# A planned three-stage kernel: where the copies of gate's and val's blocks run, when down 2's first job is made, and how the planner books its transfers

## Chip, core and metric

The kernel runs on one core of one Trainium2 chip. The metric is the device time of one execution in microseconds, given as the median of several runs.

## The reference, cut to what matters

```
x   = attention(q, k, v, omega)            # 2304 tokens x 512, kernelized attention, 4 x 8 heads
h   = x @ w_in                             # 512 -> 2048              "up 1"
x   = (h * sigmoid(h)) @ w_out             # 2048 -> 512              "down 1"
g   = x @ w_gate ; v = x @ w_val           # 512 -> 1536, twice       "up 2"
out = (g * sigmoid(g) * v) @ w_out2        # 1536 -> 512              "down 2"
```

All of it is in float32, so a matrix product is made from three products of rounded float32 (fp32r) parts: a value is split into a high part (a copy that rounds) and a low part (the value less its high part).

## The kernel before

After attention, the four large products run one after the other on TensorE: up 1, down 1, up 2, down 2. Each is a 2 x 2 block product with seven products in place of eight (`PROD`, `ORDER`), so each operand is needed as seven blocks, four of them or fewer straight from memory and the others sums of these.

**Tiles.** Up 2 walks 36 tiles n in the order of `up_order`: for each pair i of weights (gate i and val i, i = 0 to 5) and each of three column ranges s, gate's tile and then val's. One tile is seven products of six matmuls (128 x 128 by 384 columns). Products of neighbouring tiles are interleaved: product 1 of tile n+1 runs between product 7 and product 3 of tile n. Between products, `copy` (line 1123) moves a bank of PSUM to another on ScalarE, and a later product starts on that bank; `add` (line 1180), `post` (lines 1147 and 1164) and `put` (line 1132) finish a block and store it to `g_d`. Each result sits in one of ten slots (`f_s`) from its ScalarE copy until its store has landed.

**Weights.** They come as 64-bit words, and `conv_job` turns one block of weights into operands. A job has two loads (line 330), then for each half a step on ScalarE (`first`, line 352) and two on VectorE (`shift`, line 359, and `low`, line 366), then four sums on GpSimd (line 385). A job of in, gate or val goes on to four copies `hi` and four subtractions `lo` (line 432): the copies of parts 1 and 2 (512 columns each) run on VectorE (line 417), those of part 0 (256 columns) and part 3 (512 columns) on ScalarE (line 419). A job of out or out2 (`down_job`) instead stores its seven blocks to memory in three stores (line 449), and the down product loads them later (line 1285). `weave` interleaves the tail of one job with the head of the next. In up 2 the jobs stand in the order down 0, gate 1, val 1, down 1, gate 2, val 2, down 2, and so on to gate 5, val 5, down 5; gate 0 and val 0 were made in up 1 and are loaded from memory.

**Buffers.** A job takes two raw buffers (`f_raw`), two `f_c`, one `f_sum` and, for gate or val, two of six weight slots (`f_w`). Gate 0 and val 0 hold four of the weight slots when up 2 begins. The other two lie where the raw columns of the last range of x are (`T_AT`) and come free when `x_prep(1, 2)` has been emitted (`close_z`, called from `hook2`); gate 0's two come free after tile 4. The raw, `f_c` and `f_sum` buffers lie in `fa`, where down 1's operands lie before (`ZP`).

**The order of the work** is written by a planner when the kernel is built. `clk` holds an expected time for each engine, `T` one for each result. Between two products `flush` emits what it believes ready: results' work first, then the streams z, split, wd, x and conv, each no further ahead than its `ahead`. Each engine then runs its own instructions strictly in the order in which they were emitted, SyncE (all transfers) too, and waits in front of the first one that isn't ready. So the books decide the order, and real waits decide the time. A transfer is booked by `dma_cost` as bytes / 350e3 us, one after the other, plus 3.0 us.

Of the kernel before, what the change touches and what calls it, by code (L numbers as in the profile page):

```python
# [42 lines left out]
def kernel(  # L43
# [15 lines left out]
    P = 128  # L59
# [18 lines left out]
    N = 384  # L78
    NSB = NT // (2 * N)
    FP = (w_in.shape[0], w_gate.shape[0])  # L80
# [20 lines left out]
    def cut(t, o, n):  # L101
        return t[:, o : o + n]
# [36 lines left out]
                return  # L139
            self.q.append((x, clk["PE"] if t is None else t))  # L140

    clk = {e: 0.0 for e in ("PE", "ACT", "DVE", "POOL", "SP", "dma", "slot")}
    T = {}
    fixed = {"ACT": (0.21, 0.00081), "DVE": (0.15, 0.00106), "POOL": (0.25, 0.0021), "COPY": (0.1, 0.0006)}

    def cost(kind, n):
        a, b = fixed[kind]
        return a + b * n

    class Op:  # L150
# [22 lines left out]
        def emit(self):  # L173
            t = max(clk[self.eng], self.ready())
            clk["slot"] = 0.0
            clk["end"] = t + self.cost
            self.fn()
            if self.eng == "SP":
                clk["SP"] = t + 0.3
                clk["dma"] = max(t, clk["dma"]) + self.cost  # L180
                end = clk["dma"] + 3.0
            else:
                clk[self.eng] = end = t + self.cost
            for k in self.outs:
                T[k] = end
            if self.then is not None:
                self.then(end)

    def dma_cost(nbytes):
        return nbytes / 350e3  # L190

    urgent = []
    maker = {}
# [123 lines left out]
    f_s = Free("s", s_slots)  # L317
# [5 lines left out]
    def conv_job(kind, i, dram=None, side=False):  # L323
        b = {}
        key = lambda *k: (kind, i, *k)

        def load(h):
            def go():
                b["r", h] = r = f_raw.take()
                nc.sync.dma_start(out=r.bitcast(U32), in_=wsrc[kind][i, h])  # L330

            def then(end):

                if kind == "out2":
                    T[key("r", h)] = end + 6.0

            return Op("SP", dma_cost(P * 4096), go, outs=[key("r", h)], slots=(f_raw, 1), then=then)

        def word(h, w):
            return b["r", h].bitcast(U32).rearrange("p (c w) -> p c w", w=2)[:, :, w]  # L340
# [60 lines left out]
        def done(t):  # L401
            f_c.give(b["c", 0], t)
            f_c.give(b["c", 1], t)
            f_sum.give(b["S"], t)
# [5 lines left out]
        def hi(k):  # L410
            def go():
                if ("w", 0) not in b:
                    b["w", 0], b["w", 1] = f_w.take(), f_w.take()
                if side:
                    nc.gpsimd.tensor_scalar(dst(0, k), src(k), 1.0, 1.0, op0=ALU.mult, op1=ALU.mult)
                elif k in (1, 2):
                    nc.vector.tensor_copy(dst(0, k), src(k))
                else:
                    nc.scalar.activation(dst(0, k), src(k), AF.Copy)

            n = 256 * (parts[k][1] - parts[k][0])
            eng, c = ("DVE", cost("COPY", n)) if k in (1, 2) else ("ACT", cost("ACT", n))
            if side:
                eng, c = "POOL", cost("POOL", n)
            return Op(
                eng, c, go, ins=[key(*x) for x in after[k]], outs=[key("hi", k)],
                slots=lambda: None if ("w", 0) in b else (f_w, 2),
            )
# [13 lines left out]
        def store(a, z, src, ins):  # L442

            b["stores"] = 3

            def go():
                o = dram(a, z)
                t = src()
                nc.sync.dma_start(out=o, in_=t.rearrange("p (o c) -> p o c", c=256) if len(o.shape) == 3 else t)
                b["stores"] -= 1  # L450
                if not b["stores"]:
                    done(clk["end"] + 2.0)

            return Op("SP", dma_cost(P * (z - a) * 1024), go, ins=[key(*x) for x in ins], outs=[key("d", a)])

        half = [load(0), load(1), first(0), first(1), shift(0), low(0), shift(1), low(1)]
        if dram is not None:
# [51 lines left out]
    def down_job(m, i):  # L509
        k = DNK[m]  # L510
        return conv_job(
            k, i, dram=lambda a, z: wd_d[k][a:z, :, i * 256 : (i + 1) * 256].rearrange("o p c -> p o c")
        )
# [34 lines left out]
    def x_prep(m, s, raws, temps, eng, early=False, before=None, after=(), then=None):  # L548
# [9 lines left out]
        def load(j, n):  # L558
            k, h = n

            def go():
                r[n, j] = t = raws(j, 2 * k + h)
                if m == 0:
                    t0 = (2 * s + h) * N
                    for c, a, z, _, _ in runs(t0, t0 + N):
                        o = t0 + a - c * S
                        nc.sync.dma_start(out=t[:, a:z].bitcast(F32), in_=x_d[c][2 * k + j][:, o : o + z - a])
                else:
                    nc.sync.dma_start(out=t.bitcast(F32), in_=x2_d[s, 2 * k + h, j])

            if m:
                ins = [("x2", s, 2 * k + h, j), *after]
            else:
                t0 = (2 * s + h) * N
                ins = [("xd", c, 2 * k + j) for c, *_ in runs(t0, t0 + N)]
            if before is not None:
                ins = ins + [("x", m, before, "lo", n, j) for n in ("B11", "T1", "T2", "B21", "B22", "T3", "T4")]
            return Op("SP", dma_cost(P * N * 4), go, ins=ins, outs=[key(n, j)])

        def hi(name, of, j, after):  # L580
            def go():
# [494 lines left out]
    def up_phase(m, seq, hook):  # L1076
# [50 lines left out]
        def put(n, c, t, key):  # L1127
            i, kind, s = seq[n]
            f = i + (FP[m] if c & 2 else 0)

            def go():
                nc.sync.dma_start(out=g_d[m][s, c & 1, f], in_=t)
                f_s.give(t, clk["end"] + 2.0)

            soon("SP", dma_cost(P * N * 4), go, ins=[key], outs=[("g", m, s, c & 1, f)])

# [144 lines left out]
    def split_load(take, n, src, key, slots, ins=(), parts=1):  # L1281


        def load():
            nc.sync.dma_start(out=cut(take()[1], 0, n).bitcast(F32), in_=src)

        def hi(o, w):
            h, l = (cut(t, o, w) for t in take())
            nc.scalar.activation(h, l.bitcast(F32), AF.Copy)

        def lo(o, w):
            h, l = (cut(t, o, w) for t in take())
            nc.vector.tensor_sub(l, l.bitcast(F32), h.bitcast(F32))  # L1293

        def then(end):
            T[key("r")] = end + 2.0

        ops = [Op("SP", dma_cost(P * n * 4), load, ins=ins, outs=[key("r")], slots=slots, then=then)]
        w = n // parts
        for o in range(0, n, w):  # L1300
            end = [key()] if o + w == n else []
            ops += [
                Op("ACT", cost("ACT", w), lambda o=o: hi(o, w), ins=[key("r")], outs=[key("hi", o)]),
                Op("DVE", cost("DVE", w), lambda o=o: lo(o, w), ins=[key("hi", o)], outs=[key("lo", o), *end]),
            ]
        return ops

    def zload(m, s, n, k, after=()):
        fp = FP[m]
        a, h = HB[n]  # L1310
        f = a * fp + 2 * k

        def go():
            nc.sync.dma_start(
                out=ZP[n](768 * k, 768).rearrange("p (f n) -> p f n", f=2).bitcast(F32),
                in_=g_d[m][s, h, f : f + 2].rearrange("f p n -> p f n"),
            )

        return Op(
            "SP", dma_cost(2 * P * N * 4), go, ins=[("g", m, s, h, f), ("g", m, s, h, f + 1), *after], outs=[("z", m, s, n, k)],  # L1320
            guard=lambda: not len(streams["conv"]),
        )

    def down_phase(m, Wd, hook, until=None):
# [67 lines left out]
        def out_(s, c, e, t, key):  # L1392

            k, h = divmod(c, 2)

            def go():
                if m == 0:
                    nc.sync.dma_start(out=x2_d[s, c, e], in_=t)
                else:
                    t0 = (2 * s + h) * N  # L1400
                    nc.sync.dma_start(out=outT[(2 * k + e) * P : (2 * k + e + 1) * P, t0 : t0 + N], in_=t)
                f_s.give(t, clk["end"] + 2.0)

            soon("SP", dma_cost(P * N * 4), go, ins=[key], outs=[("x2", s, c, e)])

# [133 lines left out]
    def more():  # L1539

        f_c.give(extra_c)
        f_raw.give(extra_raw)
# [82 lines left out]
    for _ in d1:  # L1625
        pass
    f_w.q = deque(sorted(f_w.q, key=lambda x: x[1]))
    streams["x"].extend(x_prep(1, 2, lambda j, c: cut(ra, T_AT + (4 * j + c) * N, N), True, "DVE"))
    jobs = [down_job(1, 0)]
    for i in range(1, FP[1]):  # L1630
        jobs += [conv_job("gate", i), conv_job("val", i), down_job(1, i)]

    conv2 = weave(*jobs)
    seq2 = up_order(("gate", "val"), FP[1], False, False)
# [2 lines left out]

    def hook2(n, p):
        if n == 0 and p == 1:
            more()  # L1640
            streams["conv"].ahead = 0.8
            streams["conv"].extend(conv2)
        if not len(streams["x"]):
            close_z()
        if n == len(seq2) - 5 and p == 1:
            streams["wd"].extend(wd_ops2)
            streams["z"].extend(z_first(1, "B11", "B12"))
            streams["split"].extend(next(d2))
# [56 lines left out]
```

## Time and profile before

| | us |
|---|---|
| median of 3 runs | 840.74 (839.5 to 844.63) |
| the profiled execution, its own time | 842.8 |
| its span, first to last instruction | 841.0 |
| TensorE matmul busy | 819.3 |
| VectorE busy | 623.3 |
| ScalarE busy | 549.0 |
| GpSimd busy | 167.3 |

A span is one execution on the hardware profiler's clock; the time around it (1.8 us here) is start and end. Stages by the order of lines in the trace: attention to 118 us, up 1 to 294 us, down 1 to 459.5 us, up 2 to 714 us, then down 2.

### The profile page before, as it was taken

The numbers are of one execution on the slowest core, as the hardware profiler recorded it, in microseconds if no ns is written. First come the engines' busy times: TensorE is split into PE (matmuls) and PEld (weight loads), VectorE is DVE, ScalarE is ACT, GpSimd is POOL, SyncE is SP. The second block draws the span as 40 slices with busy tenths as digits, with TensorE's granted clock in tenths as the row PEclk, the third lists the DMA queues.
The fourth block names the chain that finished last, engine by engine and source line by source line (L and its number), as shares of the span: only waits on it lengthen the run. The fifth ranks groups of instructions, "written<-read, shape, count | busy, mean of one in ns | idle before, by whom it ended". The sixth has DMA issues, their size and how long they took to land.

```text
span 841.0 us, 18097 instructions
## 1 busy us (share of the span) xinstructions
PE 819.3 (97%) x6889; PEld 795.4 (95%) x6889; DVE 623.3 (74%) x1016; ACT 549.0 (65%) x1166; POOL 167.3 (20%) x204
## 2 busy tenths in 40 slices
PE   8999899999999999999999998999999999999998
PEld 7888789999899999999998997999999999999998
DVE  4888777667663699895999988574757548997772
ACT  6999878866677866454567865555556547755552
POOL 0477741035441000000000035121314010000000
PEclk9999999999999999999999999999999999999999
DMA  8688956669899977528415657362627168764502
GB/s 282 190 272 279 280 192 229 202 199 323 287 335 337 354 273 215 161 64 240 148 63 188 206 157 232 120 212 97 227 87 236 55 208 281 253 207 130 175 15 76
DMA packets 110119, 170.08 MB, mean 202 GB/s; under 512 B 9424, under 2 KB 94032, under 8 KB 110032
## 3 DMA queue, kind: packets, MB, share of 16 engines
q1 hardware_dynamic: 109808, 168.69, 61.2%
q8 instruction: 54, 0.88, 0.4%
q14 instruction: 33, 0.27, 0.1%
q10 hardware_dynamic: 224, 0.23, 0.1%
HBM read 107.02 MB, written 61.87 MB: 201 GB/s over the span
## 4 chain that ended last, share of the span: by engine, by line
PE 77%; DMA 7%; DVE 5%; ACT 5%; issue 3%; POOL 2%; SPq 0%; ACTq 0%; DVEq 0%; POOLq 0%
PE ps L1106 35%; PE ps L1485 32%; PE ps L760 4%; PE ps L804 2%; DMA fa<-in_moe_w_out 2%; PE ps L820 2%; PE ps L851 2%; POOL fa L385 2%; DMA wd_out<-fa 2%; ACT kq L776 2%; DMA g_d<-fa 1%; DVE fa L366 1%; ACT ps L1123 1%; ACT fa L1147 1%; DVE ra L432 1%
## 5 line engine op out<-in xcount | busy, mean ns | idle before, releaser
L385 POOL TENSOR_TENSOR fa<-fa 128x256 f32<-128x256 f32 x124 | 107.8, 884 | 494.0 <-DVE fa L366 283.3
L1106 PE MATMUL ps<-ra 128*128 128x384 f32 x840 | 148.3, 328 | 7.0 <-ACT ps L1123 6.4
L1106 PE MATMUL ps<-rb,ra 128*128 128x384 f32 x840 | 146.2, 327 | 2.9 <-ACT ps L1123 2.9
L1106 PEld LDWEIGHTS ps<-ra 128*128 128x128 f32 x840 | 137.6, 189 | 9.9 <-ACT ps L1123 8.9
L1106 PE MATMUL ps<-rc,ra 128*128 128x384 f32 x840 | 145.7, 326 | 1.1 <-ACT ps L1123 1.0
L1106 PEld LDWEIGHTS ps<-rb,ra 128*128 128x128 f32 x840 | 137.7, 189 | 4.3 <-ACT ps L1123 4.1
L1106 PEld LDWEIGHTS ps<-rc,ra 128*128 128x128 f32 x840 | 137.7, 189 | 2.1 <-ACT ps L1123 2.0
L1123 ACT ACTIVATE ps<-ps 128x384 f32<-128x384 f32 x180 | 85.1, 476 | 66.7 <-PE ps L1106 62.9
L1180 DVE TENSOR_TENSOR fa<-fa,ps 128x384 f32<-128x384 f32 x120 | 66.3, 552 | 81.6 <-ACT ps L1123 58.6
L1340 ACT ACTIVATE ra<-fa 128x768 fp32r<-128x768 f32 x87 | 73.1, 843 | 63.4 <-PE ps L1485 57.3
L1344 DVE TENSOR_TENSOR ra<-fa,ra 128x768 fp32r<-128x768 f32 x87 | 83.1, 957 | 20.2 <-ACT ra L1340 18.1
L1485 PE MATMUL ps<-ra,rb 128*128 128x384 f32 x528 | 87.5, 326 | 0.5 <-DVE rb L1293 0.5
L1485 PEld LDWEIGHTS ps<-ra,rb 128*128 128x128 f32 x528 | 86.0, 189 | 0.8 <-DVE rb L1293 0.8
L776 ACT ACTIVATE kq<-ps,nb 128x128 f32<-128x128 f32 x288 | 79.4, 405 | 7.9 <-DVE nb L774 7.6
L1485 PE MATMUL ps<-ra,rc 128*128 128x384 f32 x486 | 80.9, 327 | 1.4 <-DVE ra L1344 1.4
L1485 PEld LDWEIGHTS ps<-ra,rc 128*128 128x128 f32 x486 | 79.0, 189 | 2.3 <-DVE ra L1344 2.1
L1485 PE MATMUL ps<-ra 128*128 128x384 f32 x486 | 80.3, 326 | 0.0
L1485 PEld LDWEIGHTS ps<-ra 128*128 128x128 f32 x486 | 79.2, 189 | 0.0
L352 ACT ACTIVATE fa<-fa 128x512 f32<-128x512 f32 x65 | 53.8, 828 | 22.5 <-DMA fa<-in_moe_w_gate 5.7
L1364 DVE TENSOR_TENSOR fa<-ra,fa 128x768 f32<-128x768 f32 x63 | 60.1, 954 | 0.7
L1147 ACT ACTIVATE fa<-fa 128x384 f32<-128x384 f32 x84 | 43.6, 519 | 24.8 <-DVE fa L1180 24.7
L366 DVE SCALAR_TENSOR_TENSOR fa<-fa 128x512 uint32<-128x512 uint32 x65 | 55.0, 846 | 0.7
(108 smaller groups left out, 1086.0 us busy)
## 6 DMA issues: line engine op xcount, KB each, us to landing
g_d<-fa SPq DMA_DIRECT2D x168, 192.0 KB, 4.1
fa<-g_d SPq DMA_DIRECT2D x42, 384.0 KB, 4.5
ra<-g_d SPq DMA_DIRECT2D x42, 384.0 KB, 3.9
fa<-in_moe_w_out SPq DMA_DIRECT2D x28, 512.0 KB, 5.2
fa<-in_moe_w_in SPq DMA_DIRECT2D x16, 512.0 KB, 5.3
wd_out<-fa SPq DMA_DIRECT2D x12, 512.0 KB, 3.2
fa<-in_moe_w_gate SPq DMA_DIRECT2D x12, 512.0 KB, 4.0
fa<-in_moe_w_val SPq DMA_DIRECT2D x12, 512.0 KB, 5.1
```

The costliest lines, as they stand in the source:

```text
L352: nc.scalar.activation(c, word(h, 1).bitcast(F32), AF.Prelu, scale=2.0**-112, alpha=-(2.0**32))
L366: nc.vector.scalar_tensor_tensor(c, word(h, 0), 29, c, op0=ALU.logical_shift_right, op1=ALU.bitwise_or)
L385: f(blk(f"S{n}"), blk(l), blk(r))
L776: nc.scalar.activation(e[:, g // 2, g % 2, h * M : (h + 1) * M], x[:, g, :], AF.Exp, bias=nb[:, g : g + 1])
L1106: nc.tensor.matmul(woven(ps[b][:, :N]), cut(l, j * P, P), halves(cut(r, j * N, N)), start=start and c == 0, stop=stop and c == 5, skip_gro ...
L1123: nc.scalar.activation(out() if callable(out) else out, src, AF.Copy)
L1147: nc.scalar.activation(b["t"], src, AF.Silu)
L1180: nc.vector.tensor_add(t, t if in_place else p5[n], ps[bank_][:, :N])
L1340: nc.scalar.activation(ops[s, p, k][0], src(), AF.Copy)
L1344: nc.vector.tensor_sub(l, src(), h.bitcast(F32))
L1364: (nc.gpsimd if eng == "POOL" else nc.vector).tensor_sub(z(PLACE[to]), z(PLACE.get(l, l)), z(PLACE.get(r, r)))
L1485: nc.tensor.matmul(woven(ps[BANKS[p] + e][:, :N]), cut(a, e * P, P), halves(b), start=p in FIRST and i == 0 and c == 0, stop=p in LAST and ...
```

## The change

- Parts 1 and 2 of gate's and val's jobs are copied on ScalarE; `in` keeps VectorE for them.
- Up 2's jobs stand in the order gate 1, val 1, down 0, gate 2, val 2, down 1, to gate 5, val 5, down 4, down 5.
- Before up 2's jobs are planned, each raw, `f_c` and `f_sum` buffer is booked free when the last subtraction of down 1 that reads its place is expected to end (`last_read`); the extra `f_c` and raw buffer are in the lists from the start (`more()` goes).
- A transfer is booked by its kind: a wait of 1.55 us before it, a time per byte, and a delay to landing. A slot whose store is under way is booked free at the landing (`clk["landed"]`) in place of the issue's end plus 2.0 us. A load of in or out counts as ready 1 us after landing, of gate or val 2.5 us after, of out2 6 us after as before. This concerns up 1, down 1, up 2 and down 2.

```diff
@@ class Op, emit
-            clk["end"] = t + self.cost
+            if self.eng == "SP":
+                took, lag = self.cost
+                clk["SP"] = t + 0.35
+                clk["dma"] = max(t + 1.55, clk["dma"]) + took
+                clk["end"] = clk["landed"] = clk["dma"] + lag
+            else:
+                clk["end"] = t + self.cost
             self.fn()
             if self.eng == "SP":
-                clk["SP"] = t + 0.3
-                clk["dma"] = max(t, clk["dma"]) + self.cost
-                end = clk["dma"] + 3.0
+                end = clk["landed"]
@@
-    def dma_cost(nbytes):
-        return nbytes / 350e3
+    RATE = {"rows": (1.71e-6, 0.85), "parts": (2.63e-6, 0.79), "words": (4.21e-6, 0.71), "g": (3.48e-6, 1.27), "wd": (3.16e-6, 1.02)}
+
+    def dma_cost(nbytes, kind="rows"):
+        a, b = RATE[kind]
+        return nbytes * a, b
@@ conv_job, load
-                if kind == "out2":
+                if kind != "out2":
+                    T[key("r", h)] = end + (1 if kind in ("in", "out") else 2.5)
+                else:
                     T[key("r", h)] = end + 6.0
@@ conv_job, hi
-                elif k in (1, 2):
+                elif k in (1, 2) and kind == "in":
                     nc.vector.tensor_copy(dst(0, k), src(k))
                 else:
                     nc.scalar.activation(dst(0, k), src(k), AF.Copy)
@@ put, out_ and the stores of a job
-                f_s.give(t, clk["end"] + 2.0)
+                f_s.give(t, clk["landed"])
@@ before up 2
+    def last_read(o, n):
+        ks = range(FP[0] // 2)
+        t = [(C_AT + 768 * k, T["d", 0, "lo", NSB - 1, 4, k]) for k in ks]
+        t += [(C_AT + 3072 + 768 * k, T["d", 0, "lo", NSB - 1, 7, k]) for k in ks]
+        return max(x for a, x in t if a < o + n and o < a + 768)
+
+    f_c.q = deque((cut(fa, o, 512), last_read(o, 512)) for o in (XR_AT, *(C_AT + i * 512 for i in range(3))))
+    f_raw.q = deque((cut(fa, o, 1024), last_read(o, 1024)) for o in (XR_AT + 512, R_AT + 1024, R_AT))
+    f_sum.q = deque([(cut(fa, SUM_AT, 1024), last_read(SUM_AT, 1024))])
@@
-    jobs = [down_job(1, 0)]
+    jobs = []
     for i in range(1, FP[1]):
-        jobs += [conv_job("gate", i), conv_job("val", i), down_job(1, i)]
+        jobs += [conv_job("gate", i), conv_job("val", i), down_job(1, i - 1)]
+    jobs.append(down_job(1, FP[1] - 1))
@@ hook2
-            more()
```

## Rows read from the trace of the kernel before

**Rows 1.** The page: busy time and share of the span.

```profile
PE 819.3 (97%) x6889; PEld 795.4 (95%) x6889; DVE 623.3 (74%) x1016; ACT 549.0 (65%) x1166; POOL 167.3 (20%) x204
```

**Rows 2.** TensorE's waits in up 1, then in 436 to 545, then after: total, times, longest.

```profile
PE ps L1106 <- ACT ps L1123: 4.9, 7, 1.1
...
PE ps L1106 <- ACT ps L1123: 5.3, 6, 1.7
PE ps L1485 <- DVE ra L1344: 1.4, 2, 1.1
PE ps L1106 <- DVE ra L432: 0.5, 1, 0.5
...
PE ps L1485 <- DVE rb L1293: 0.5, 1, 0.5
```

**Rows 3.** Timeline of TensorE at the start of up 2: start, duration, [wait before].

```profile
496.94 1.24 PE L1106 MATMUL ps<-ra 128*128 128x384 f32 x6 [1.46 <-ACT ps L1123]
...
508.86 1.24 PE L1106 MATMUL ps<-rb,ra 128*128 128x384 f32 x6 [0.80 <-ACT ps L1123]
...
510.91 1.89 PE L1106 MATMUL ps<-ra 128*128 128x384 f32 x10 [0.48 <-DVE ra L432]
...
515.45 3.19 PE L1106 MATMUL ps<-ra 128*128 128x384 f32 x18 [1.67 <-ACT ps L1123]
...
526.26 1.24 PE L1106 MATMUL ps<-rc,ra 128*128 128x384 f32 x6 [0.73 <-ACT ps L1123]
```

**Rows 4.** Busy time by stretch: length, PE, PEld, DVE, ACT, POOL, granted clock, DMA share, GB/s.

```profile
500.00:510.00 10.00, 9.20 (x56) 8.75 (x55) 9.90 (x18) 4.83 (x10) 5.11 (x6) 1.00 0.62 189
510.00:520.00 10.00, 7.85 (x47) 7.17 (x45) 9.02 (x16) 6.38 (x13) 3.85 (x4) 1.00 0.59 185
...
540.00:581.00 41.00, 41.00 (x255) 41.00 (x254) 25.81 (x48) 22.95 (x46) 10.03 (x12) 1.00 0.49 158
```

**Rows 5.** Timeline of SyncE's queue at the start of up 2: start, time, count.

```profile
483.32 5.45 SPq L449 DMA_DIRECT2D wd_out<-fa  x2
...
489.41 2.58 SPq L1132 DMA_DIRECT2D g_d<-fa  x4
```

**Rows 6.** Timeline of ScalarE at the start of up 2.

```profile
494.57 0.49 ACT L1123 ACTIVATE fa<-ps 128x384 f32<-128x384 f32 x1 [2.98 <-PE ps L1106]
...
496.40 0.48 ACT L1123 ACTIVATE ps<-ps 128x384 f32<-128x384 f32 x1
496.81 0.40 ACT L419 ACTIVATE ra<-fa 128x256 fp32r<-128x256 f32 x1
```

**Rows 7.** Transfers by line: count, KB each, median us from issue to landing.

```profile
g_d<-fa SPq DMA_DIRECT2D x168, 192.0 KB, 4.1
```

**Rows 8.** Groups by line and shape in 541 to 582: busy, mean ns | idle before.

```profile
L366 DVE SCALAR_TENSOR_TENSOR fa<-fa 128x512 uint32<-128x512 uint32 x6 | 4.8, 800 | 0.0
L432 DVE TENSOR_TENSOR ra<-fa,ra 128x512 fp32r<-128x512 f32 x6 | 4.3, 732 | 0.0
L359 DVE TENSOR_SCALAR fa<-fa 128x512 uint32<-128x512 uint32 x6 | 2.5, 418 | 1.9 <-ACT fa L352 1.9
L417 DVE CAST ra<-fa 128x512 fp32r<-128x512 f32 x4 | 1.7, 421 | 0.0
L419 ACT ACTIVATE ra<-fa 128x512 fp32r<-128x512 f32 x2 | 1.3, 629 | 0.0
```

**Rows 9.** The line of the VectorE copies over the whole span: count, ns, first and last start.

```profile
L417 DVE CAST ra<-fa x30: 415/421/752, 171.9 to 669.2; 128x512 fp32r<-128x512 f32 x30
```

**Rows 10.** Timeline of SyncE's queue at the end of up 2.

```profile
675.89 0.37 SPq L449 DMA_DIRECT2D wd_out<-fa  x1
...
676.90 1.48 SPq L1314 DMA_DIRECT2D fa<-g_d  x2
...
689.19 0.91 SPq L1314 DMA_DIRECT2D fa<-g_d  x2
```

**Rows 11.** Timeline of VectorE at the end of up 2: down 2's first low part.

```profile
687.65 0.95 DVE L1344 TENSOR_TENSOR ra<-fa,ra 128x768 fp32r<-128x768 f32 x1
```

**Rows 12.** ScalarE's waits in front of line 352 in up 1: total, times, longest.

```profile
ACT fa L352 <- DMA fa<-in_moe_w_in: 5.5, 4, 1.8
```

More of the change, by code (lines that the diff above doesn't have):

```diff
@@ L140, in give @@
             self.q.append((x, clk["PE"] if t is None else t))
-    clk = {e: 0.0 for e in ("PE", "ACT", "DVE", "POOL", "SP", "dma", "slot")}
+    clk = {e: 0.0 for e in ("PE", "ACT", "DVE", "POOL", "SP", "dma", "slot", "landed")}
     T = {}
@@ L332, in then @@
             def then(end):
-                if kind == "out2":
+                if kind != "out2":
+                    T[key("r", h)] = end + (1 if kind in ("in", "out") else 2.5)
+                else:
                     T[key("r", h)] = end + 6.0
-            return Op("SP", dma_cost(P * 4096), go, outs=[key("r", h)], slots=(f_raw, 1), then=then)
+            return Op("SP", dma_cost(P * 4096, "words"), go, outs=[key("r", h)], slots=(f_raw, 1), then=then)
         def word(h, w):
@@ L421, in hi @@
             n = 256 * (parts[k][1] - parts[k][0])
-            eng, c = ("DVE", cost("COPY", n)) if k in (1, 2) else ("ACT", cost("ACT", n))
+            eng, c = ("DVE", cost("COPY", n)) if k in (1, 2) and kind == "in" else ("ACT", cost("ACT", n))
             if side:
@@ L451, in go @@
                 if not b["stores"]:
-                    done(clk["end"] + 2.0)
-            return Op("SP", dma_cost(P * (z - a) * 1024), go, ins=[key(*x) for x in ins], outs=[key("d", a)])
+                    done(clk["landed"])
+            return Op("SP", dma_cost(P * (z - a) * 1024, "parts"), go, ins=[key(*x) for x in ins], outs=[key("d", a)])
         half = [load(0), load(1), first(0), first(1), shift(0), low(0), shift(1), low(1)]
@@ L577, in load @@
                 ins = ins + [("x", m, before, "lo", n, j) for n in ("B11", "T1", "T2", "B21", "B22", "T3", "T4")]
-            return Op("SP", dma_cost(P * N * 4), go, ins=ins, outs=[key(n, j)])
+            return Op("SP", dma_cost(P * N * 4, "g"), go, ins=ins, outs=[key(n, j)])
         def hi(name, of, j, after):
@@ L1296, in then @@
             T[key("r")] = end + 2.0
-        ops = [Op("SP", dma_cost(P * n * 4), load, ins=ins, outs=[key("r")], slots=slots, then=then)]
+        ops = [Op("SP", dma_cost(P * n * 4, "wd"), load, ins=ins, outs=[key("r")], slots=slots, then=then)]
         w = n // parts
@@ L1319, in zload @@
         return Op(
-            "SP", dma_cost(2 * P * N * 4), go, ins=[("g", m, s, h, f), ("g", m, s, h, f + 1), *after], outs=[("z", m, s, n, k)],
+            "SP", dma_cost(2 * P * N * 4, "g"), go, ins=[("g", m, s, h, f), ("g", m, s, h, f + 1), *after], outs=[("z", m, s, n, k)],
             guard=lambda: not len(streams["conv"]),
@@ L1401, in go @@
                     nc.sync.dma_start(out=outT[(2 * k + e) * P : (2 * k + e + 1) * P, t0 : t0 + N], in_=t)
-                f_s.give(t, clk["end"] + 2.0)
+                f_s.give(t, clk["landed"])
             soon("SP", dma_cost(P * N * 4), go, ins=[key], outs=[("x2", s, c, e)])
```

## The prediction

> **What bounds the kernel now.** The page comes first: TensorE's matmuls are busy for 819.3 of 841.0 us [rows 1]. No edit here changes a matmul, so all there is to win or lose is the time in which TensorE stands still. The second view is therefore TensorE's own waits, stage by stage [rows 2]: 4.9 us in up 1, 7.2 us from the end of down 1 into up 2 (5.3 + 1.4 + 0.5), and 0.5 us after that. That is 12.6 us, 1.5% of the time. The third view is the timeline of TensorE where up 2 starts [rows 3]: five waits between 495 and 527 us, 1.46 + 0.80 + 0.48 + 1.67 + 0.73 = 5.14 us. The change's new order and its copies work at this place, so these waits are the sum's first term. The fourth view, busy time by stretch [rows 4], says why they are there: from 500 to 520 us VectorE is busy for 9.90 and 9.02 of each 10 us, ScalarE only for 4.83 and 6.38. Later, in 540 to 581, TensorE never waits, VectorE has 25.81 of 41 and ScalarE 22.95 of 41.
>
> Four of the five waits are put down to line 1123, a bank copy on ScalarE, though ScalarE is half idle. The copy is late for what is queued ahead of it or for what its own slot and bank wait for. The first wait can be followed. SyncE's queue spent 5.45 us on two stores of down 0's blocks, held by their sums, and the stores of results behind them left from 489.41 [rows 5]. Such a store lands 4.1 us after its issue [rows 7], so at about 493.5 its slot is free, and ScalarE, which had stood for 2.98 us in front of a copy into a slot, went on at 494.57; the bank copy behind it came at 496.40 [rows 6], and TensorE's 1.46 us wait ended at 496.94 [rows 3]. The trace names TensorE as the releaser of that copy, but the product it copies had long ended; I read it as the slot. The wait of 0.48 us is val 1's operands coming late. The other three, 3.20 us, lie where gate 1's tail, all of val 1, down 1's head and gate 2's head crowd onto VectorE.
>
> **The order of jobs.** Before, down 0 goes first and gate 1 and val 1 follow. Gate 1 can't be copied before the last range of x is done and its two weight slots come free; its first copy is at 496.81 [rows 6]. Val 1 waits for gate 0's slots, free after tile 4, about the same time. The new order doesn't move these two gates; it moves what can be done ahead of them. The heads of gate 1 and val 1 need only raw and `f_c` buffers, and four `f_c` and three raw ones are there. What then leaves VectorE between 497 and 514: gate 1's second half, 0.42 + 0.80 = 1.22 us; val 1's first shift, 0.42; four copies of 0.42, 1.68 [rows 8]. That is 3.3 us out of a stretch that was over 90% full. Down 0 takes down 1's place there, at the same price. The stores of down 0, which held SyncE's queue, come after x is done and VectorE has room. So the wait of 1.46 goes and the 0.48 goes; of the other 3.20 I take half. The gain is 1.46 + 0.48 + 1.60 = 3.5 us; its ends are 0 (all come back with another job) and 5.1.
>
> **The copies.** Line 417 has 30 instructions [rows 9]; ten belong to in 3 to 7 and stay, so twenty move (ten jobs, two each). One costs VectorE 0.42 us and ScalarE 0.63 [rows 8]: 8.4 us leave the one, 12.6 us come to the other, over 255 us. In the steady part, that is four copies in 41 us: ScalarE goes from 22.95 to 25.5 of 41, VectorE from 25.8 to 24.1 [rows 4]. This lies beside TensorE's work as long as no bank copy is pushed past its slack. The cover is thin right after a weight slot comes free, when four copies are ready at once; if it fails, see the first rival. Its ends are 0 and 8.4 us (worked out there); I take 0.3, near 0, since the nearest row is the steady part with no wait.
>
> **The tail.** The down jobs run one job later now, so after val 5, which still waits for gate 4's slots, come the rest of down 4 and all of down 5. Before, the last store is at 675.89 and down 2's first loads follow at 676.90, since they may not be planned while the conv stream has work [rows 10]. An out2 load is booked ready some 10 us after its issue (1.55 + 2.2 + 0.7 + 6), so I take the first loads 10 to 14 us later. Behind them, the next pair left at 689.19 anyway [rows 10], held by gate 5's and val 5's own results. So only the first two operands of down 2 are late; the first low part, 0.95 us of VectorE at 687.65 [rows 11], moves to about 699, 15 us before down 2 starts. VectorE is the tight engine there (TensorE's one wait, 0.5 us, is for it [rows 2]), so up to two low parts, 1.9 us, could come back as a wait. Its ends are 0 and 1.9; I take 0.3, as there is idle time between.
>
> **Buffers booked to their last read.** No instruction is added. The raw loads of gate 1 come out at the start of up 2 as down 0's did, and SyncE meets the same real waits. The extra pair in the list from the start lets a third raw load go with the first two. No cost, no gain of its own; if a load were issued ahead of its buffer's release, the x loads and stores behind it on SyncE would stand, which is what the booked times avoid.
>
> **The books by kind.** They change the order in up 1, down 1 and up 2. A 512 KB weight load was ready 4.5 us after issue (1.5 + 3.0) and now is at 4.5 + 1 for in and out, + 2.5 for gate and val. In up 1 ScalarE stood 5.5 us in front of line 352 for loads of in [rows 12]; this shrinks. It needn't reach TensorE: up 1's waits are 4.9 us in all [rows 2], with conv work that ends well before up 1 does. I bound the books by these waits, a gain of 4.9 us or a loss as large, and take 0, because I can't tell which order comes out.
> A slot under store was free 2.56 us after issue in the books (0.56 + 2.0) and now is at 1.55 + 0.34 + 0.85 = 2.74 with an empty queue, but a landing takes 4.1 us [rows 7]. So the new book is still 1.4 us short. The Trainium skill, page "DMA: Bandwidth & Descriptors", section "Anatomy of one DMA — SWDGE (gpsimd) path", has about 2.0 us fixed plus the bytes at 436 GB/s for a transfer issued from GpSimd; an estimate by it for 192 KB is 2.45 us. By that the new book would be long enough, and the slot waits in up 1 would go as well, a gain nearer to the upper end; the row, for this kernel's own queue, decides.
>
> **The sum.** 3.5 - 0.3 - 0.3 = 2.9 us less. The profiled execution took 842.8 us (span 841.0 and 1.8 around), 2.1 above the median of 840.74, so it would come to 839.9, and the median to **837.8**.
>
> **Rivals.** *The copies burst (slower).* When a gate's slots come free, the next val's four copies are ready together: 0.40 + 3 x 0.63 = 2.29 us on ScalarE [rows 6, 8], before it was 0.40 + 0.63 = 1.03. A bank copy has two products' time: 255 matmuls in 41.00 us [rows 4] make 0.965 us for six, so 1.93 us, less its own 0.48 [rows 6], 1.45 us of slack. 1.03 fits, 2.29 is 0.84 too long. Over ten jobs, 8.4 us: 837.8 + 8.4 = 846.2. From 0.29 us a job on the kernel is slower than before. Against it: conv work is emitted at most 0.8 us ahead, so seldom more than two copies pass at once, and bank copies are put in between.
> *The tail decides:* two low parts come late, 837.8 + 1.6 = 839.4.
> *It doesn't do what it says:* the slots stay booked short and the crowd only changes its members; 5.1 us of waits remain and the two small costs come on top: 841.3.
> *The books decide:* up 1's 4.9 us go too, 832.9, or double, 842.7.
>
> **How the numbers follow.** Forecast 0.45, burst 0.12, tail 0.10, no effect 0.18, books better 0.10, books worse 0.05. About 1% (8.4 us) is what a measurement of this kernel can tell from no change. Faster by that is below 832.3: only the better books with all five waits gone, 837.8 - 4.9 - 1.6 = 831.3, so 0.08. Slower by that is above 849.1: only a burst together with worse books, 0.07. The range runs from 831.5 (that lower end) to 845 (most of the burst), leaving out a little of both.
>
> **What the profile would show.** Right: the waits of [rows 3] shrink to under 2 us; line 417 has ten instructions left and line 419 fifty, at 0.63 us; gate 1's line 352 steps precede down 0's; VectorE in 500 to 520 is under 9 of 10 us; SyncE has no down store before 497. Wrong: waits for line 1123 that recur every 41 us after 540 (the burst), a wait for line 1344 or 1293 after up 2 ends (the tail), or up 1 with more than 4.9 us (the books). What would make the forecast wrong most easily is a new order in up 1 or down 1 that I couldn't derive from the trace.

## The result, and the profile after

| | before | after |
|---|---|---|
| median of 6 runs | 840.69 | 831.51 (830.65 to 833.37) |
| the profiled execution, its own time | 842.8 | 830.65 |
| its span | 841.0 | 828.9 |

The ratio is 0.9891, 95% interval 0.9869 to 0.9912: 9.2 us less, 7.4 to 11.0. The prediction had 2.9 us less. In the lines below, each line number is larger by 9 than in the kernel before wherever the books are new (line 1123 is 1132, 352 is 361, 1180 is 1189, 417 is 426, 419 is 428, 432 is 441).

The page of the kernel after, busy time and share [rows 1]:

```profile
PE 817.5 (99%) x6889; PEld 796.1 (96%) x6889; DVE 621.1 (75%) x996; ACT 561.5 (68%) x1186; POOL 163.7 (20%) x204
```

Twenty instructions have gone from VectorE to ScalarE, and ScalarE is 12.5 us busier, as worked out. TensorE's waits after, in up 1 (first line) and from 436 to 545 us; there are none from 545 to the end [rows 2]:

```profile
PE ps L1115 <- ACT ps L1132: 1.6, 3, 0.7
...
PE ps L1115 <- ACT ps L1132: 1.7, 3, 1.0
PE ps L1494 <- DVE ra L1353: 1.4, 2, 1.1
```

Listed waits fell from 4.9 to 1.6 us in up 1 and from 5.8 to 1.7 in up 2; the 1.4 at the end of down 1 stayed and the 0.5 in down 2 went. The timeline of TensorE after, up 2's waits [rows 3]:

```profile
456.52 2.22 PE L1115 MATMUL ps<-ra 128*128 128x384 f32 x12 [0.41 <-ACT ps L1132]
459.03 1.24 PE L1115 MATMUL ps<-rb,ra 128*128 128x384 f32 x6 [0.29 <-ACT ps L1132]
505.18 3.19 PE L1115 MATMUL ps<-ra 128*128 128x384 f32 x18 [1.03 <-ACT ps L1132]
```

Of the five waits of [rows 3] one is left: counted in matmuls from the start of up 2, it stands where the one of 1.67 us stood, and is now 1.03. Busy time by stretch, after (columns as in [rows 4]; up 2 begins 5.6 us earlier now):

```profile
490.00:500.00 10.00, 10.00 (x64) 10.00 (x63) 9.40 (x17) 7.58 (x16) 3.26 (x4) 1.00 0.48 145
500.00:510.00 10.00, 8.96 (x55) 8.56 (x54) 7.41 (x12) 5.92 (x12) 3.77 (x4) 1.00 0.61 186
510.00:520.00 10.00, 10.00 (x64) 10.00 (x63) 7.04 (x13) 6.64 (x15) 3.48 (x4) 1.00 0.74 240
540.00:581.00 41.00, 41.00 (x254) 41.00 (x254) 24.73 (x45) 24.90 (x50) 10.31 (x13) 1.00 0.49 159
```

From 500 to 510 us VectorE is less busy than before, but what stood there has moved ahead: gate 1's and val 1's copies now run from 488 to 498 us, and from 490 to 500 VectorE is about as full as it was (9.40 of 10) without any wait of TensorE. So a full VectorE alone doesn't make TensorE wait. In the steady part, where ScalarE has 24.90 of 41, TensorE never waits either.

**Where the time went, by stage.** A stage runs from its first matmul in TensorE's timeline to that of the next, down 2 to the end of the span. All kernels of this study, one profiled execution each:

| kernel | median, us | against before | up 1 | up 2 | down 2 |
|---|---|---|---|---|---|
| before | 840.69 | | 173.99 | 254.13 | 127.32 |
| after | 831.51 | 0.9891 | 170.50 | 248.32 | 126.58 |
| e1 books alone | 836.55 | 0.9957 | 171.12 | 252.13 | 126.53 |
| e2 order alone | 839.95 | 1.0007 | 174.69 | 253.71 | 127.36 |
| e3 copies alone | 840.96 | 1.0013 | 173.61 | 255.31 | 127.29 |
| e4 last reads alone | 840.44 | 1.0003 | 173.15 | 252.21 | 127.29 |
| e5 after, old order | 833.75 | 0.9922 | 169.94 | 251.96 | 126.55 |
| e6 after, old copies | 833.58 | 0.9918 | 170.99 | 249.14 | 127.34 |
| e7 after, old last reads | 831.75 | 0.9895 | 170.89 | 248.30 | 126.56 |
| e8 after, old books | 839.05 | 0.9988 | 172.90 | 253.08 | 127.37 |
| e9 order + load lag of gate, val | 835.49 | 0.9948 | 171.25 | 249.07 | 127.56 |
| e10 after, short lag | 834.79 | 0.9944 | 171.23 | 253.05 | 126.61 |
| e11 load lag of in, out alone | 840.02 | 1.0000 | 172.22 | 256.31 | 127.40 |
| e12 after, longer lag | 834.46 | 0.9931 | 172.88 | 248.33 | 126.52 |

The 95% intervals of the ratios reach 0.0013 to 0.0019 to either side (after: 0.0022). A profiled execution can lie off its kernel's median: 2.1 us above it before, 1.9 in e2, 2.9 in e10 and 3.2 in e11, at most 1.2 to either side in the others; so the stages of these four are on the long side. Down 1 took 165.95 us in all but e9 (166.93), e10 (166.33) and e11 (166.80). The profiled spans differ by 12.1 us, and 2.1 of these lie in attention, ahead of everything the change touches: TensorE's first matmul of up 1 is at 119.61 before and 117.55 after, and at 117.80 to 119.31 in the other kernels. The stages that the change touches give 3.5 + 5.8 + 0.7 = 10.0 us of one execution against another, the medians 9.2.

Before, e2, e3, e4 and e8 plan up 1 with the same books, and their edits touch up 2 alone: ScalarE, VectorE and GpSimd run the same lines in the same order up to the start of up 2. Their up 1 takes 172.90 to 174.69 us, mean 173.7. After, e1, e5, e6 and e7 share the new books and take 169.94 to 171.12, mean 170.7. So a single execution of up 1 says no more than about 1 us either way, and the books' part there is 3.0 us.

### The profile page after: what moved, and what is told of

Its sections match the earlier page's. It is cut to its first block, busy times and chain, and to the rows that moved or that the text cites. A ratio compares the mean times of both kernels' runs of the same rounds, so it can differ in the third digit from the quotient of the medians.

```text
span 828.9 us, 18089 instructions
## 1 busy us (share of the span) xinstructions
PE 817.5 (99%) x6889; PEld 796.1 (96%) x6889; DVE 621.1 (75%) x996; ACT 561.5 (68%) x1186; POOL 163.7 (20%) x204
## 4 chain that ended last, share of the span: by engine, by line
PE 85%; DMA 4%; ACT 4%; DVE 4%; issue 2%; POOL 0%; SPq 0%; ACTq 0%; DVEq 0%; POOLq 0%
PE ps L1115 42%; PE ps L1494 32%; PE ps L769 4%; PE ps L813 2%; DMA fa<-in_moe_w_out 2%; PE ps L829 2%; PE ps L860 2%; ACT kq L785 2%; DMA fa<-in_moe_w_in 1%; DMA ra<-wd_out 1%; PE ps L885 1%; DVE nb L783 1%; DVE fa L375 1%; DMA g_d<-fa 1%; ACT ps L1132 1%
## 5 line engine op out<-in xcount | busy, mean ns | idle before, releaser
L394 POOL TENSOR_TENSOR fa<-fa 128x256 f32<-128x256 f32 x124 | 103.9, 853 | 496.0 <-DMA ra<-x_d 208.0
L375 DVE SCALAR_TENSOR_TENSOR fa<-fa 128x512 uint32<-128x512 uint32 x65 | 58.5, 900 | 0.6
```

The source lines that it names most:

```text
L375: nc.vector.scalar_tensor_tensor(c, word(h, 0), 29, c, op0=ALU.logical_shift_right, op1=ALU.bitwise_or)
L394: f(blk(f"S{n}"), blk(l), blk(r))
```

## The experiments

### One part of the change at a time (e1 to e4)

Each keeps from the diff only what its name says. e1 keeps the hunks of `emit`, `RATE`, `dma_cost`, the load's `then` and `clk["landed"]`; of the others these lines were added to the kernel before:

```diff
e2  -    jobs = [down_job(1, 0)] ...
e2  +    jobs += [conv_job("gate", i), conv_job("val", i), down_job(1, i - 1)] ...
e3  -                elif k in (1, 2):
e3  +                elif k in (1, 2) and kind == "in":
e4  +    f_c.q, f_raw.q, f_sum.q = (... last_read ...)
e4  -            more()
```

> The kernel before with the transfers' books by kind alone (old order, old copies, no booked last reads). If the books made up 1 shorter: up 1 takes about 170.5 us in place of 174.0, TensorE's waits there 1.6 in place of 4.9, and the kernel is 3.5 us faster or more. If the order of the jobs made all of up 2's gain, up 2 stays at 254 us here. Rival (the books do nothing, up 1's gain is chance between two executions): within 1 us of before, up 1 at 174.

Measured: 836.55 us, ratio 0.9957 (0.9939 to 0.9975), the only part that does anything alone. Up 1 takes 171.1 us, with 2.8 us of TensorE's waits. The rival falls. Up 2 is 2.0 us shorter too, with one large wait in place of five. Timeline of ScalarE in e1:

```profile
497.81 0.48 ACT L428 ACTIVATE ra<-fa 128x256 fp32r<-128x256 f32 x1
503.28 0.63 ACT L428 ACTIVATE ra<-fa 128x512 fp32r<-128x512 f32 x1 [4.98 <-POOL fa L394]
503.81 0.47 ACT L1132 ACTIVATE ps<-ps 128x384 f32<-128x384 f32 x1
```

And of TensorE in e1:

```profile
504.34 2.14 PE L1115 MATMUL ps<-rb,ra 128*128 128x384 f32 x6 [3.05 <-ACT ps L1132]
```

ScalarE stands 4.98 us in front of val 1's copy of part 3, for the sums on GpSimd; a bank copy is queued behind it and TensorE waits 3.05 us for that. The same pattern returns in e2, e8 and e10: a conversion step that was emitted ahead of its input blocks the bank copy behind it. After this wait TensorE's granted clock also falls for a while, to half (1.2 in place of 2.4 GHz). Busy time by stretch in e1 (columns as in [rows 4]):

```profile
500.00:510.00 10.00, 6.95 (x32) 6.65 (x32) 8.90 (x17) 4.45 (x9) 5.45 (x6) 0.83 0.67 205
```

About eleven matmuls then start 0.32 us apart in place of 0.1625, which is some 1.7 us that no row of waits lists; the last section comes back to it.

> The kernel before with the new order of up 2's jobs alone (gate 1, val 1, down 0, ...). As the prediction has it: up 2's five waits lose 1.46 + 0.48 + 1.6 us, 3 us faster in all, up 2 near 250.5 us, up 1 unchanged at 174. Rival (the crowd only changes its members): up 2 at 254 us and the kernel within 1 us of before.

Measured: 839.95 us, ratio 1.0007 (0.9993 to 1.0020). Up 2 takes 253.71 us in the profiled execution, so neither the 3 us of the prediction nor quite the rival's picture: the 1.46 and 0.48 us waits did go, and a new one came. Timeline of ScalarE in e2, at the start of up 2:

```profile
463.35 0.73 ACT L352 ACTIVATE fa<-fa 128x512 f32<-128x512 f32 x1 [1.44 <-DMA fa<-in_moe_w_gate]
```

Timeline of TensorE in e2, the wait behind it and two later ones:

```profile
465.73 2.11 PE L1106 MATMUL ps<-rb,ra 128*128 128x384 f32 x6 [1.96 <-ACT ps L1123]
509.14 1.24 PE L1106 MATMUL ps<-rb,ra 128*128 128x384 f32 x6 [0.51 <-ACT ps L1123]
515.48 3.19 PE L1106 MATMUL ps<-ra 128*128 128x384 f32 x18 [2.18 <-ACT ps L1123]
```

Gate 1 is the first job now, and its load is booked ready 4.5 us after issue. ScalarE's first step for it is emitted by that and stands 1.44 us for the load, and TensorE waits 1.96 us. Down 0 in the same place had been booked 6 us later still, so the old order didn't have this. The clock falls behind the 1.96 us wait too (0.83 on average from 460 to 470 us); but e2's three executions at a mean clock of 1.000 took 839.6 to 839.7 us, with 839.72 before in the same round, so the fall isn't what hides the gain.

> The kernel before with gate's and val's copies on ScalarE alone. As the prediction has it: 0 to 0.3 us slower by itself. If VectorE's load at the start of up 2 was the cause of the waits: 2 us faster or more, VectorE below 9 of 10 us in 500 to 520. If the copies burst on ScalarE: up to 8 us slower, with new waits for the bank copies every 41 us.

Measured: 840.96 us, ratio 1.0013 (0.9999 to 1.0028). Up 2 is 1.2 us longer than before. VectorE's load as the cause isn't cleared by this run, since VectorE is still busy for 9.40 of 10 us from 500 to 510 (8.10 in the next ten); the changed kernel, with 9.40 from 490 to 500 and no wait, speaks against it. The burst didn't come either: from 540 us on TensorE has one wait of 0.63 us, at 562.

> The kernel before with the buffers booked to their last read in down 1 alone (and the extra pair in the lists from the start). As the prediction has it: no difference beyond 0.5 us. Rival: the pair in the lists from the start lets gate 1's head go earlier, and 1 us or more of up 2's waits goes.

Measured: 840.44 us, ratio 1.0003 (0.9990 to 1.0016). Nothing, as expected. In its profile the 1.46 us wait is absent: here the three sums of down 0 took 2.93 us on GpSimd in place of 4.94, SyncE was held by down 0's stores for 3.44 us in place of 5.45 [rows 5], and the stores of results left at 486.57 us. Of the six kernels with the old order, four have this wait (before, e3, e5, e11, with sums of 4.94 to 4.96 us) and two lack it (e1 and e4, 2.94 and 2.93). Each was profiled once, so it is open whether the kernel or the single execution decides.

### The changed kernel with one part undone (e5 to e8)

The same hunks, taken back one at a time.

> The changed kernel with the old order of up 2's jobs (down 0 first). The single parts gave up 2 2.0 us less (books), 0.4 less (order), 1.2 more (copies), 1.9 less (last reads), against 5.8 less together. Theory A, the parts need each other and the order is the one that lets them: up 2 goes back to 252 us or more, the kernel is 4 us or more slower than the changed one (about 835.5). Theory B, the order does nothing: within 1 us of 831.5.

Measured: 833.75 us, ratio 0.9922 (0.9906 to 0.9939). Up 2 is 3.6 us longer, the median 2.2 us. Theory B falls; theory A has the direction, but neither of its figures is reached (252 us and 4 us), and the interval overlaps that of the changed kernel. The old order also brings the wait at 495 back, and this time its releaser is named. Timeline of ScalarE in e5:

```profile
488.90 0.49 ACT L1132 ACTIVATE fa<-ps 128x384 f32<-128x384 f32 x1 [2.86 <-DMA g_d<-fa]
```

TensorE's waits of up 2 in e5, from the timeline, behind the two at its start (0.41 and 0.28):

```profile
491.17 1.24 PE L1115 MATMUL ps<-ra 128*128 128x384 f32 x6 [1.16 <-ACT ps L1132]
504.27 1.89 PE L1115 MATMUL ps<-ra 128*128 128x384 f32 x10 [0.81 <-DVE ra L441]
508.43 3.19 PE L1115 MATMUL ps<-ra 128*128 128x384 f32 x18 [1.29 <-ACT ps L1132]
512.12 2.22 PE L1115 MATMUL ps<-rb,ra 128*128 128x384 f32 x12 [0.50 <-ACT ps L1132]
```

The copy into a slot waits 2.86 us for a store to land, after SyncE had been held 5.46 us by down 0's stores, as in [rows 5, 6]. Val 1's late operands are back as well (0.81).

> The changed kernel with the copies of parts 1 and 2 back on VectorE. By the prediction (copies leave a full VectorE at gate 1 and val 1): up 2 1 to 2 us longer than 248.3. By what they did alone (1.2 us longer with them): up 2 1 us shorter, the kernel at 830.5.

Measured: 833.58 us, ratio 0.9918 (0.9901 to 0.9936). Up 2 is 0.8 us longer and has one more wait (0.52 us at 502.48); the median is 2.1 us above the changed kernel's, with intervals that overlap. That wait stands in front of the same matmul of up 2 as the 0.80 of [rows 3]; with the new order and the old copies it is there (e2, e6, e9, 0.51 to 0.52), with the new order and the new copies it is not (after, e7, e8, e10, e12). So with the new order the copies take this wait away; alone (e3) they gained nothing. The profiled execution is also 0.5 us longer in up 1 and 0.8 behind the last matmul of down 2 (4.63 us to the end of the span in place of 3.86). VectorE is busy for 9.35 us between 500 and 510 here, 7.41 in the changed kernel.

> The changed kernel without the buffers booked to their last read (and with the extra pair handed out only when up 2's jobs are planned). By the prediction nothing: within 0.5 us of 831.5. By what they did alone: up 2 about 2 us longer, 833.4.

Measured: 831.75 us, ratio 0.9895 (0.9876 to 0.9913), up 2 at 248.30 (after: 248.32). No effect.

> The changed kernel with the old books of transfers. By the sum of the single parts: up 1 back to 174, down 2 back to 127.3, up 2 at 253.4, so 839.5 or so. By the prediction (order and copies work without the books): up 2 at 250.5, so 836.5.

Measured: 839.05 us, ratio 0.9988 (0.9976 to 1.0001). The sum of the single parts was right, the prediction's own figure wrong: without the books, order, copies and last reads are worth 1.3 us of 840.3, not clear of nothing (the interval reaches 1.0001). Its timeline has e2's wait, 1.93 us at 463.32, behind ScalarE's 1.38 us for gate 1's load.

### Which line of the books the order needs (e9, e10)

```diff
 # e9, in the kernel before with the new order        # e10, in the changed kernel
+ elif kind in ("gate", "val"):                       - end + (1 if kind in ("in", "out") else 2.5)
+     T[key("r", h)] = end + 2.5                      + end + 1
```

> The kernel before with the new order and one line of the books: loads of gate and val count as ready 2.5 us later. In the new order with the old books ScalarE stood 1.44 us in front of gate 1's first step for its load and TensorE then 1.96 us for the bank copy behind. Theory A (the order needs the later booking of its first loads): ScalarE's wait for gate's load at the start of up 2 is gone, TensorE's too, up 2 at 251.5 us or less, the kernel 2 us faster than before. Rival B (the rest of the books is what it takes): up 2 stays at 253.5.

Measured: 835.49 us, ratio 0.9948 (0.9932 to 0.9964). Up 2 takes 249.07 us: 5.0 of its 5.8 us, with the old copies and the rest of the books old. Theory A holds for the pair; the later booking without the new order was not run (e1 has it together with all the other books: up 2 at 252.13). ScalarE doesn't wait for a load of gate at the start of up 2, and TensorE's waits there are the 0.41 and 0.28 that the kernel before has as well. Up 1 takes 171.25 us in this execution, which wasn't expected: gate 0 and val 0 are made there.

> The changed kernel with loads of gate and val counted as ready 1 us after landing, like in and out, in place of 2.5. Theory A: gate 1's first step is emitted ahead of its load again and TensorE waits at the start of up 2, up to 2 us; up 2 at 249.5 to 250.5. Rival B (the later landing in the books of kinds is enough): up 2 at 248.3, no wait there.

Measured: 834.79 us, ratio 0.9944 (0.9927 to 0.9962). Up 2 is 253.05 us, 4.7 more than after, in an execution 2.9 us above the median; by the median the kernel is 3.3 us slower than after. Timeline of ScalarE in e10:

```profile
460.75 0.71 ACT L361 ACTIVATE fa<-fa 128x512 f32<-128x512 f32 x1 [1.53 <-DMA fa<-in_moe_w_gate]
```

Timeline of TensorE in e10:

```profile
463.12 1.24 PE L1115 MATMUL ps<-rb,ra 128*128 128x384 f32 x6 [2.04 <-ACT ps L1132]
510.67 4.86 PE L1115 MATMUL ps<-ra 128*128 128x384 f32 x18 [2.05 <-ACT ps L1132]
```

1.5 us in one booked time bring both back, the wait at the start and a longer last one (2.05 in place of 1.03). That is 2.8 us of the 4.7; behind the second wait the clock falls again, which is another 1.7 (18 matmuls take 4.86 us there, 3.19 after). Busy time by stretch in e10:

```profile
510.00:520.00 10.00, 9.34 (x47) 9.34 (x48) 5.99 (x10) 4.56 (x10) 4.44 (x6) 0.83 0.77 264
```

e10's four executions at a mean clock of 1.000 took 834.5 to 834.8 us, so 3 us of loss stand without this. Rival B falls.

### Up 1 (e11, e12)

```diff
 # e11, in the kernel before                           # e12, in the changed kernel
+ elif kind in ("in", "out"):                          - end + (1 if kind in ("in", "out") else 2.5)
+     T[key("r", h)] = end + 1.0                       + end + 2.5
```

> The kernel before with loads of in and out counted as ready 1 us later, nothing else. Theory A (up 1's gain is ScalarE no longer standing in front of a conversion for its load): ScalarE's 9.7 us of such waits in up 1 fall to about 5, up 1 takes 170.5 to 171.5 us, the kernel 2.5 to 3 us faster. Rival B (the order of stores and of the other transfers does it): up 1 stays at 173 to 174.7.

Measured: 840.02 us, ratio 1.0000 (0.9984 to 1.0015). Up 1 takes 172.22 us, between the two theories; ScalarE still stands 7.7 us for loads there (2.9 of them for gate). Up 2, with the old order, got longer in this execution, which lies 3.2 us above the median: 256.31 us, with a wait of 2.36 us at 479 in which ScalarE stood 3.7 us for gate 1's second load. Neither theory is shown.

> The changed kernel with loads of in and out counted as ready 2.5 us after landing as well. If ScalarE's 5.0 us of waits for loads in up 1 still cost TensorE its 1.6 us there: up 1 at 169.5 us or less, 1 us faster than the changed kernel. If later conversions hold the buffers longer: no gain, or up 1 longer.

Measured: 834.46 us, ratio 0.9931 (0.9915 to 0.9947), slower than the changed kernel. ScalarE's waits for loads in up 1 are gone, and up 1 is longer, 172.88 us, for one block came too late. TensorE's timeline in e12:

```profile
239.47 7.67 PE L1115 MATMUL ps<-ra 128*128 128x384 f32 x34 [1.97 <-DVE ra L441]
```

The clock falls behind this wait as well (0.83 from 238 to 248 us). So a later booking buys freedom for ScalarE's queue and pays with lateness, and 2.5 us is too much for in and out. None of the versions beats the changed kernel.

## Why the prediction came out as it did

The direction was right, and at the start of up 2 the place and part of the mechanism; the size was not: 2.9 us said, 9.2 measured. The measured 831.51 us lies at the very end of the range named (831.5 to 845); that it still lies inside is luck. Nearest came the rival in which the books decide for the better (832.9, chance 0.10), but that rival had only up 1's waits go: up 1 gave 3.0 to 3.5 us, and the rest came from what the books do to the order in up 2. Nor is 1% the least that can be told from no change: the intervals above tell 0.2%. Term by term:

- **The order, 3.5 us.** What it does to two waits was read rightly: the slot wait behind down 0's stores and val 1's late operands go with it (e2, e9), and come back with the old order (e5, which names the store as releaser; e1 and e4 show that the slot wait can also be absent in the old order). VectorE's load, given as why the waits are there, is not enough for one: it is about as full after (9.40 of 10), only earlier, so that the sign "VectorE in 500 to 520 is under 9" came true for another reason. The step that failed is "it moves what can be done ahead of them": I looked at the heads of gate 1 and val 1 as free work and left out that ScalarE's first step may stand in front of its load. Alone the order is worth 0.4 us of up 2; together with gate's and val's loads booked 2.5 us later, 5.0 (e9); and taken out of the changed kernel, 3.6 of up 2 and 2.2 of the time (e5), so that beside the new books the 3.5 of the sum is about its size.
- **The books, 0, with 4.9 us either way.** This is the term that was mis-sized. They are worth 3.0 us in up 1 (means of five executions each) and they are what makes the order pay in up 2. "I can't tell which order comes out" was true, but the rows were there: ScalarE's waits for loads [rows 12], and the loads' median time from issue to landing, 4.0 to 5.3 us against the 4.5 booked. In the kernel before:

```profile
fa<-in_moe_w_in SPq DMA_DIRECT2D x16, 512.0 KB, 5.3
fa<-in_moe_w_gate SPq DMA_DIRECT2D x12, 512.0 KB, 4.0
fa<-in_moe_w_val SPq DMA_DIRECT2D x12, 512.0 KB, 5.1
```

A later booked time shortens a wait in front of a conversion, and a bank copy can be queued behind that wait.
- **How up 1's 3.0 us come about** is only half settled. The waits in front of line 352 for loads and for freed buffers fell, from 13.8 us before (5.5 + 2.2 + 1.5 + 0.5 for loads, 4.1 for sums on GpSimd) to 5.0. But e9 has 6.8 + 2.5 and up 1 at 171.25, e11 has 7.7 and 172.22, e12 has almost none and 172.88. Their sum isn't what up 1 follows. Which steps of the new order matter was not separated. ScalarE's waits in front of this line in up 1, before (beside the 5.5 of [rows 12]) and after:

```profile
ACT fa L352 <- POOL fa L385: 4.1, 4, 1.6
ACT fa L352 <- DMA fa<-in_moe_w_gate: 2.2, 1, 2.2
ACT fa L352 <- DMA fa<-in_moe_w_out: 1.5, 1, 1.5
ACT fa L352 <- DMA fa<-in_moe_w_val: 0.5, 1, 0.5
...
ACT fa L361 <- DMA fa<-in_moe_w_out: 3.3, 4, 1.9
ACT fa L361 <- DMA fa<-in_moe_w_in: 1.7, 3, 0.7
```

- **The copies, 0.3 us of loss.** With the rest in place they gain 0.8 us of up 2 (e6); in the old order and with the old books up 2 was 1.2 us longer with them (e3). The durations were right; the wait that they take away (0.80 in [rows 3], 0.52 in e6) was not in this term. The line of the old copies and of ScalarE's, after:

```profile
L426 DVE CAST ra<-fa x10: 402/423/447, 169.1 to 235.8; 128x512 fp32r<-128x512 f32 x10
L428 ACT ACTIVATE ra<-fa x50: 395/615/669, 169.6 to 658.3; 128x512 fp32r<-128x512 f32 x35, 128x256 fp32r<-128x256 f32 x15
```

The burst did not happen: gate 1's and val 1's eight copies lie one or two at a time between bank copies from 488 to 498 us, and no wait recurs after 540.

- **The tail, 0.3 us of loss.** The moves came, the loss didn't. SyncE's queue after, down 5's last store, then down 2's first loads [rows 10]:

```profile
673.29 0.39 SPq L458 DMA_DIRECT2D wd_out<-fa  x1
673.73 1.57 SPq L1323 DMA_DIRECT2D fa<-g_d  x2
```

Counted back from the start of down 2 (713.68 and 702.32 us), these loads leave 28.6 us ahead in place of 36.8: 8.2 us later, where 10 to 14 was said. Down 2 has no listed wait and is 0.7 us shorter: the 0.5 us wait [rows 2] is gone in every kernel with the new books by kind and there in every other, so it is the books' doing and not the tail's. In e6 too it is gone (122.69 us from down 2's first matmul to its last, as after, 123.48 before).
- **The last reads, 0.** Right (e4, e7).
- **The slot's book.** The row's 4.1 us to a landing against the new book's 2.74 was a rival's ground. No kernel took this line alone. Slot waits were not what was left: the wait that remains, 1.03 us, is a silu on ScalarE standing for VectorE's sum, then a conversion step of 0.64 us (0.42 of it in the chain), then the bank copy. Chain of waits after:

```profile
503.18 0.48 DVE fa L1189
503.65 0.02 issue
503.68 0.53 ACT fa L1156
504.20 0.42 ACT fa L361
504.62 0.03 issue
504.65 0.49 ACT ps L1132
505.14 0.04 issue
505.18 6.85 PE ps L1115 x40
```

Gains of single edits don't add here. In up 2 they are 2.0 us (books), 0.4 (order), -1.2 (copies) and 1.9 (last reads, of which the time and e7 show nothing) against 5.8 together; in the time 3.6, -0.6, -1.1 and -0.3 against 9.2, and of the last three each interval takes in no change.

## What to carry to other kernels

Where a planner writes the order and each engine keeps it, the step that a queue stops at costs more than the step itself: ask of every moved step whether its input can be there when its turn comes, and what is queued behind. A booked time that is too early is paid by whoever stands behind the step, one that is too late by whoever needs the result, so the right one lies between (here 1.5 us too little for gate and val cost 3.3 us, e10, and 1.5 us too much for in and out 3.0, e12). Try the parts of a change together and one at a time: the order, worth nothing alone, is worth about 2 us beside the new books.

## What the runs showed that was not expected

A wait costs more than its row says. After, 36 matmuls from 473.76 to 479.61 us take 0.1625 us each, so up 2's 1512 take 245.7 us. Up 2 took 248.32 with 1.7 us of listed waits in three, and 254.13 before with 5.8 in seven: 0.9 and 2.6 us are in no row. The starts of the single matmuls show where they are. A row counts its idle time from the modelled end of the matmul before, 0.33 us after that one's start, not from the usual 0.1625, which leaves out 0.16 us; and the second matmul behind the wait starts another 0.10 us late. So each wait costs some 0.27 us beyond its row (before there is an eighth, of 0.14 us, too short to be listed). That is 1.7 of up 2's 5.8 us, which a sum of listed waits could not show.

Long waits can also cost clock. The granted clock fell to half right behind a wait of TensorE in five traces: e1 (3.05 us), e2 (1.96), e8 (1.93), e10 (2.05) and e12 (1.97), at some 1.7 us each. Behind three others as long it did not: 2.18 in e2, 2.04 in e10, 2.36 in e11. From up 1 on the changed kernel has no wait over 1.12 us, and its six executions have a mean clock of 1.000.

Three sums of 128 x 256 on GpSimd took 4.94 us before and 2.93 in e4, with the same lines in the same order around them on VectorE; a single sum took 0.72 to 3.14 us. Before, one sum took 3.14 us while VectorE's instructions beside it went on at 0.58 us each; in e4 the sums took about 1 us each, and three of VectorE's instructions beside them 1.08 us in place of 0.55. The Trainium skill, page "SBUF — State Buffer", section "Who interferes with whom", says that a VectorE instruction with two SBUF inputs and a GpSimd instruction that reads SBUF shut each other out. VectorE was full of such instructions at the time, and in each of the two traces one side gave way, which fits, but no run here isolates it.
